# Row-halved attention scores in one PSUM ring, q and k transposed by DMA from tile 6 on, masks built by VectorE

## The chip, the cores and the metric

One core of a Trainium2 chip. The metric is the device time of one execution in microseconds. In a run on a chip, the kernel to be judged and the kernel before are executed in turn on the same chip. A **ratio** is the mean time of one kernel's fast runs over that of the other's fast runs of the same rounds, so it is not quite the ratio of the medians that stand beside it. The span of a profile, from the first to the last instruction, is about 2 us shorter than the time.

## The reference, cut to what matters

```python
scores = (q @ k.T) / sqrt(64) - slope[h] * dist      # B=4, H=8, S=768, D=64
keep   = (pos_k < 8) | ((0 <= rel) & (rel < 96))     # 8 global keys, a window of 96
a      = softmax(where(keep, scores, -1e9))
x      = (a @ v) as [B*S, 512]
out    = relu(x @ w_in)**2 @ w_out                   # w_in [512, 2048], w_out [2048, 512]
```

The 3072 rows are 24 tiles of 128. A tile's queries see only the keys of their own tile and of the one before (the 8 global keys are copied into the latter). Two tiles make a block of the second part; "s1" is x @ w_in in eight steps a block (its result is `hT`), "s2" the product with w_out, "pv" the product a @ v. In the first three tiles a "mask product" adds the distance term to the scores.

## The kernel before: the parts that matter

The kernel plans its own order. Every piece of work is an `op` with a cost, its dependencies and the ring buffer that it takes; a list scheduler puts the pieces in an order, and each engine then executes its own instructions strictly in that order. Some instructions are emitted directly, before the plan:

```python
nc.vector.memset(zero.bitcast(I32), 0)
for j in range(NT):                                   # 24 tiles
    nc.vector.memset(v_sb[j][:, :, D : D + 1], 1.0)   # column of ones beside v
make_identity(nc, ident)
load_qk(1)                                            # loads go out on POOL's queue
...                                                   # masks by POOL
load_v(0)
load_v(1)
nc.vector.tensor_copy(ident32, ident)
```

`v_sb[j]` holds 8 heads of 64 values and a 65th column of ones, with which the product `a @ v` gives the softmax's sum as well.

Scores take one product for a pair of heads: `kT` has both heads' keys on 128 partitions, `qz` has the queries in two halves padded with zeros.

```python
nc.tensor.matmul(out=sc[:, i, :, :], lhsT=kT[kj][:, p_, :],
                 rhs=qz[zi][:, p_, :, :], ...)        # 128 rows x 256 columns
```

TensorE transposes q, k and x for tiles 0 to 9, DMA transposes do it from tile 10 on. PSUM is split: 2 banks of accumulators, 3 of `hT`, 2 of scores, 1 of `po`.

The softmax here doesn't subtract the row's maximum and nothing guards it: scores larger than these inputs give would overflow.

Of the kernel before, what the change touches and what calls it, by code (L numbers as in the profile page):

```python
# [22 lines left out]
class Plan:  # L23
# [7 lines left out]

    LAG = {"PE": 0.25, "ACT": 0.15, "DVE": 0.12, "SP": 2.6, "POOLQ": 2.5, "DMA": 0.0}

# [16 lines left out]
    def run(self):  # L50
        rings = {}
        free = {e: 0.0 for e in self.LAG}
# [10 lines left out]
        while ready:  # L63
            best = None
            for o in ready:
                at = o["at"]
                if o["takes"]:
                    tag, bufs, users = o["takes"]
                    ring = rings.setdefault(tag, [])
                    if len(ring) >= bufs:  # L70
                        old = ring[-bufs]
                        if any("end" not in u for u in old):
                            continue
                        at = max([at] + [self.after(u, o["engines"]) for u in old])
                for e, cost in o["engines"].items():
                    r = (max(at, free[e]), o["key"], cost, o["n"])
                    if best is None or r < best[0]:
                        best = (r, o, e)
# [3 lines left out]
            o["start"], o["engine"], o["end"] = r[0], e, r[0] + o["engines"][e]  # L82
            free[e] = o["end"]
            if o["takes"]:
                rings[o["takes"][0]].append(o["takes"][2])
# [12 lines left out]
def kernel(  # L98
# [32 lines left out]
    NG = NBLK * NSTEP  # L131
    NACC = 2
    NPLAIN = 1
    NFIRST = 4
    NBIAS = 3
    JQK, JX = 10, 10
    NQ, NPAD, NKT, NQZ = 10, 8, 2 * TPB, 4
# [4 lines left out]
    ps_h = ctx.enter_context(tc.tile_pool(name="ps_h", bufs=5 - NACC, space=PSUM))  # L142
    ps_sc = ctx.enter_context(tc.tile_pool(name="ps_sc", bufs=2, space=PSUM))
    ps_o = ctx.enter_context(tc.tile_pool(name="ps_o", bufs=1, space=PSUM))
# [5 lines left out]
    q_ring = [const([P, d_model], BF16, f"q_{i}") for i in range(NQ)]  # L150
    q_pad = [const([P, NPAIR, 2, P], BF16, f"qpad_{i}") for i in range(NPAD)]
    k_ring = [const([P, d_model], BF16, f"k_{i}") for i in range(NQ)]
    v_sb = [const([P, H, D + 1], BF16, f"v_{j}") for j in range(NT)]
    kT = [const([P, NPAIR, P], BF16, f"kT_{i}") for i in range(NKT)]
    qz = [const([P, NPAIR, 2, P], BF16, f"qz_{i}") for i in range(NQZ)]
# [4 lines left out]
    E = const([P, NPAIR, 2, 2, P], BF16, "E")  # L160
    E0 = const([P, NPAIR, 2, P], BF16, "E0")
# [4 lines left out]
    zero = const([P, 4 * P], BF16, "zero")  # L166
    plan = Plan()
    NHS = 14
    E_AT = 14.0
    NWARM = 8  # L170
    HOLD = {}
# [4 lines left out]
    clock = [4.2]  # L176
# [8 lines left out]
    def swdge(name, dst, src, t):  # L185
        nc.gpsimd.dma_start(out=dst, in_=src)  # L186
        clock[0] += t
        land[name] = clock[0]

    q_tile, k_tile = {}, {}  # L190
    for j in range(NPLAIN):
        for n, src in (("q", q), ("k", k)):
            t_ = const([P, d_model], FP32, f"plain_{n}{j}")
            nc.sync.dma_start(
                out=t_.rearrange("p (h d) -> p h d", h=H),
                in_=src_rows(src, j).rearrange("h p d -> p h d"),
            )
            (q_tile if n == "q" else k_tile)[j] = t_
            land[n, j] = 4.1 + 2.1 * j + (1.05 if n == "k" else 0.0)


    def load_v(j):
        swdge(("v", j), v_sb[j][:, :, :D], src_rows(v, j).rearrange("h p d -> p h d"), 0.85)

    def load_qk(j):
        k_tile[j] = k_ring[j % NQ]
        todo = [("k", k_tile[j], k)]
        if j < JQK:
            q_tile[j] = q_ring[j % NQ]
            todo.insert(0, ("q", q_tile[j], q))  # L210
        else:
            q_tile[j] = q_pad[j % NPAD]
            s_ = src_rows(q, j).rearrange("(a e) p d -> e p a d", e=2)
            for e in range(2):
                swdge(("q", j), q_tile[j][:, :, e, e * D : (e + 1) * D], s_[e], 0.43)
        for n, dst, src in todo:
            swdge(
                (n, j), dst.rearrange("p (h d) -> p h d", h=H),
                src_rows(src, j).rearrange("h p d -> p h d"), 0.85,
            )  # L220

    def load_tile(j):
        load_qk(j)
        load_v(j)
# [17 lines left out]
    for j in range(NT):  # L242
        nc.vector.memset(v_sb[j][:, :, D : D + 1], 1.0)
    make_identity(nc, ident)
    load_qk(1)


    nc.gpsimd.iota(pbi, pattern=[[-P, 2], [-1, P]], base=0, channel_multiplier=1)
    nc.gpsimd.tensor_copy(pb, pbi)
    nc.gpsimd.affine_select(  # L250
        out=pb, in_=pb, compare_op=Alu.is_ge, fill=MASK_VAL,
        base=0, pattern=[[P, 2], [1, P]], channel_multiplier=-1,
    )
    nc.gpsimd.affine_select(
        out=pb, in_=pb, compare_op=Alu.is_ge, fill=MASK_VAL,
        base=n_local - 1, pattern=[[-P, 2], [-1, P]], channel_multiplier=1,
    )
    load_v(0)
    load_v(1)
    nc.vector.tensor_copy(ident32, ident)  # L260
    nc.vector.memset(qz[0].bitcast(I32), 0)
    nc.vector.memset(qz[1].bitcast(I32), 0)
    for h in range(H):
        nc.vector.tensor_scalar_mul(sid[h], ident, float(slopes[h] / scale))
    nc.vector.tensor_copy(pb0, pb[:, 0, :])
    nc.vector.tensor_scalar_max(
        pb0[:n_global, :], pb0[:n_global, :], float(-n_local)
    )
    nc.vector.memset(pb[:n_global, 1, :], float(-n_local))
    nc.vector.memset(qz[2].bitcast(I32), 0)  # L270
    nc.vector.memset(qz[3].bitcast(I32), 0)

    warm = ps_o.tile([P, 4 * P], FP32, name="warm", tag="po")
    for i in range(NWARM):
        nc.tensor.matmul(out=warm, lhsT=zero[:, :P], rhs=zero, start=True, stop=True)

    load_tile(2)
    load_w_in(0)
    load_tile(3)
    load_w_out(0)  # L280
    for w in range(1, NSTEP):
        load_w_in(w)
        load_w_out(w)
        if w in (3, 5):
            load_tile(NFIRST + (w - 3) // 2)
# [9 lines left out]
    def any_copy(e, dst, src):  # L295
        if e == "ACT":
            nc.scalar.copy(dst, src)  # L297
        else:
# [4 lines left out]
            ("E", pair), {"ACT": 0.65}, key=0.3 + pair, ready=E_AT,  # L303
            emit=lambda e, pair=pair: [
                nc.scalar.activation(
                    E[:, pair, :, h, :], pb, Act.Exp, scale=float(slopes[2 * pair + h])
                )
                for h in range(2)
            ],
        )  # L310
        for pair in range(NPAIR)
    ]

    def emit_E0(e, c):

        pairs = slice(2 * c, 2 * c + 2)
        nc.vector.tensor_copy(E0[:, pairs], E[:, pairs, 0])
        nc.vector.tensor_max(  # L318
            E0[:n_global, pairs], E[:n_global, pairs, 0], E[:n_global, pairs, 1]
        )  # L320
# [3 lines left out]
            ("E0", c), {"DVE": 0.6}, emit=lambda e, c=c: emit_E0(e, c), key=4 + c,  # L324
            deps=maskE[2 * c : 2 * c + 2],
        )
        for c in range(2)
# [3 lines left out]
    qz_users = [[] for _ in range(NQZ)]  # L331
    kT_users = [[] for _ in range(NKT)]
    qk_users = [[] for _ in range(NQ)]
    pad_users = [[] for _ in range(NPAD)]
# [5 lines left out]
    for j in range(NT):  # L340
# [3 lines left out]
        base = need - LEAD + 4 * (j % 2)  # L344


        if j in late:
            def emit_load(e, j=j):
                if j == JQK:
                    for i in range(NPAD):  # L350
                        nc.gpsimd.memset(q_pad[i].bitcast(I32), 0)
                load_tile(j)
            ld = plan.op(
                ("load", j), {"POOLQ": 2.6}, emit_load,
                deps=qk_users[j % NQ] + (pad_users[j % NPAD] if j >= JQK else []),
                key=base, ready=clock[0],
            )
            qk_users[j % NQ] = []
            if j >= JQK:
                pad_users[j % NPAD] = []  # L360
# [3 lines left out]
        zi, ki = j % NQZ, j % NKT  # L364
        fp = j < NPLAIN
        parts = []
        for n in ("q", "k") if j < JQK else ():
            users = []

            def emit_tr(e, j=j, n=n, fp=fp):  # L370
                pool, tag = ps_h, "hT"
                tr = pool.tile([P, NPAIR, P], FP32 if fp else BF16, name=f"tr{n}", tag=tag)
                src = (q_tile if n == "q" else k_tile)[j]
# [8 lines left out]
                ("tr", n, j), {"PE": 0.85 if fp else 0.24}, emit_tr,  # L382
                deps=[land[n, j]], key=base, ready=HOLD.get(j, 0.0),
                takes=("hT", 5 - NACC, users),
            )
            users.append(tr)
            if n == "q":
                for e_ in range(2):
                    half = slice(e_ * D, (e_ + 1) * D)

                    def emit_z(e, j=j, e_=e_, half=half, zi=zi):
                        any_copy(e, qz[zi][half, :, e_, :], tiles["tr", "q", j][half])

                    z = plan.op(
                        ("z", e_, j), {"DVE": 0.7 if fp else 0.43, "ACT": 0.57}, emit_z,
                        deps=[tr] + qz_users[zi], key=base + 0.1,
                    )
                    users.append(z)
                    parts.append(z)
            else:  # L400
                def emit_T(e, j=j, n=n, ki=ki):
                    any_copy(e, kT[ki], tiles["tr", n, j])

                c = plan.op(
# [412 lines left out]
```

## Time and profile before

| | before |
|---|---|
| time, median of 3 runs | 225.9 us (225.72 to 226.42) |
| span of the profiled run | 223.7 us |
| TensorE busy | 211.1 us, 94% |
| VectorE, ScalarE busy | 146.1 us, 123.3 us |
| granted TensorE clock, mean | 0.989 |

Lines of the timeline: the columns are start, duration, engine, source line, operation and tiles.

TensorE's first useful product starts at 4.21.

### The profile page before, as it was taken

Reading aid. Unit: us, or ns where it says so; the run is one execution under the profiler, and the core shown is the slowest. Engines: PE = TensorE matmul, PEld = TensorE weight load, DVE = VectorE, ACT = ScalarE, POOL = GpSimd, SP = SyncE. Lnnn points to the kernel's source line nnn. Section 1 sums busy time; section 2 is a strip of 40 time slices with the busy share of each in tenths; the row PEclk is TensorE's granted clock in tenths of the full one; section 3 lists DMA queues with packets and bytes.
Section 4 is the critical chain, followed back from the end, with each engine's and each line's share of the span. In section 5 each row is a group of like instructions: output and inputs, shape, how many; then the busy total and the mean of one; then the engine's idle time right before and its main releaser. Section 6 shows DMA issues by size and latency. Waiting matters only on the chain.

```text
span 223.7 us, 4803 instructions
## 1 busy us (share of the span) xinstructions
PE 211.1 (94%) x1817; PEld 151.9 (68%) x1848; DVE 146.1 (65%) x380; ACT 123.3 (55%) x225; POOL 88.0 (39%) x118
## 2 busy tenths in 40 slices
PE   6499999999999999999999999999999999999992
PEld 2388677765777777766767777776776676676750
DVE  6466857677766868757666866866756856844530
ACT  3359666674755944645644745734645644643530
POOL 8996677799978985505605000000000000000000
PEclk9979999999999999999999999999999999999998
DMA  9999999999999999998999984256524430300202
GB/s 132 102 148 199 183 197 180 175 174 169 167 146 151 152 171 169 134 214 98 163 166 129 124 118 95 67 124 95 143 54 90 131 70 13 117 11 17 94 0 94
DMA packets 115142, 27.83 MB, mean 124 GB/s; under 512 B 105776, under 2 KB 112176, under 8 KB 115120
## 3 DMA queue, kind: packets, MB, share of 16 engines
q0 software_dynamic: 79424, 13.38, 79.5%
q1 hardware_dynamic: 35696, 14.16, 32.6%
q8 instruction: 14, 0.23, 0.4%
q14 instruction: 8, 0.07, 0.1%
HBM read 27.26 MB, written 6.29 MB: 150 GB/s over the span
## 4 chain that ended last, share of the span: by engine, by line
PE 82%; POOL 6%; DVE 4%; DMA 4%; ACT 2%; issue 1%; POOLq 0%
PE acc L723 35%; PE hT L659 35%; PE sc L442 7%; PE po L549 4%; DMA win<-in_moe_w_in_dram 4%; DVE hs L692 2%; POOL v L186 1%; POOL q L186 1%; POOL k L186 1%; ACT hr L680 1%; DVE o L299 1%; POOL win L186 1%; PE trx L611 1%; POOL wout L186 1%; ACT qz L297 1%
## 5 line engine op out<-in xcount | busy, mean ns | idle before, releaser
L659 PE MATMUL hT<-xT,win 128*128 128x256 bf16 x768 | 98.6, 273 | 0.5 <-ACT xT L297 0.4
L680 ACT ACTIVATE hr<-hT 128x512 f32<-128x512 f32 x96 | 57.3, 597 | 74.7 <-PE hT L659 72.7
L723 PE MATMUL acc<-wout,hs 128*128 128x512 bf16 x353 | 94.8, 379 | 1.6
L659 PEld LDWEIGHTS <-win 128*128 128x128 bf16 x768 | 74.7, 98 | 23.4 <-DMA win<-in_moe_w_in_dram 0.7
L692 DVE TENSOR_TENSOR hs<-hr 128x512 bf16<-128x512 f32 x96 | 65.9, 687 | 25.7 <-ACT hr L680 24.3
L723 PEld LDWEIGHTS <-hs 128*128 128x128 bf16 x384 | 34.5, 98 | 22.8
L482 ACT ACTIVATE esc<-sc 128x512 bf16<-128x512 f32 x78 | 46.2, 593 | 2.4 <-PE sc L442 2.3
L442 PE MATMUL sc<-qz,kT 128*128 128x256 bf16 x176 | 35.3, 276 | 0.7 <-ACT at L482 0.4
L503 DVE TENSOR_TENSOR at<-esc,E 128x512 bf16<-128x512 bf16 x78 | 32.4, 417 | 0.1
L186 POOL DMA_DIRECT2D qpad<-in_q_dram x28 | 21.6, 800 | 23.0 <-DMA qz<-qpad 23.0
L186 POOL DMA_DIRECT2D v<-in_v_dram x24 | 22.0, 918 | 2.6 <-DVE E L318 1.7
L186 POOL DMA_DIRECT2D k<-in_k_dram x23 | 21.2, 920 | 3.1 <-PE trx L611 1.8
L575 DVE TENSOR_TENSOR x<-po,rs 128x256 bf16<-128x256 f32 x48 | 20.4, 424 | 1.7
L549 PEld LDWEIGHTS <-at 128*128 128x128 bf16 x352 | 17.2, 99 | 5.9
L574 DVE RECIPROCAL rs<-po 128x4 f32<-128x4 f32 x48 | 8.7, 180 | 18.2 <-PE po L549 17.6
L442 PEld LDWEIGHTS <-kT 128*128 128x128 bf16 x176 | 17.1, 99 | 3.1 <-DVE kT L299 0.8
L549 PE MATMUL po<-v,at 128*128 128x65 bf16 x352 | 18.8, 194 | 0.0
L299 DVE COPY o<-acc 128x512 f32<-128x512 f32 (+1 forms) x12 | 8.0, 664 | 8.2 <-PE acc L723 4.3
L297 ACT COPY o<-acc 128x512 f32<-128x512 f32 (+1 forms) x13 | 7.4, 570 | 5.3 <-PE acc L723 5.2
L297 ACT COPY qz<-trq 64x512 bf16<-64x512 bf16 x10 | 5.8, 580 | 7.5 <-DVE qz L299 5.3
L522 DVE COPY kT<-kT 128x32 bf16<-128x32 bf16 x16 | 3.4, 210 | 9.2 <-PE sc L442 9.2
L186 POOL DMA_DIRECT2D q<-in_q_dram x9 | 8.3, 924 | 1.5 <-DMA wout<-in_moe_w_out_dram 1.2
(52 smaller groups left out, 91.2 us busy)
## 6 DMA issues: line engine op xcount, KB each, us to landing
out_dram<-o SPq DMA_DIRECT2D x23, 256.0 KB, 2.5
v<-in_v_dram POOLq DMA_DIRECT2D x24, 128.0 KB, 6.7
k<-in_k_dram POOLq DMA_DIRECT2D x23, 128.0 KB, 5.7
win<-in_moe_w_in_dram POOLq DMA_DIRECT2D x8, 256.0 KB, 8.4
wout<-in_moe_w_out_dram POOLq DMA_DIRECT2D x8, 256.0 KB, 8.8
qpad<-in_q_dram POOLq DMA_DIRECT2D x28, 64.0 KB, 4.5
q<-in_q_dram POOLq DMA_DIRECT2D x9, 128.0 KB, 7.9
plain_q<-in_q_dram SPq DMA_DIRECT2D x1, 256.0 KB, 3.3
```

Of the source, the lines that this page charges most:

```text
L186: nc.gpsimd.dma_start(out=dst, in_=src)
L297: nc.scalar.copy(dst, src)
L299: nc.vector.tensor_copy(dst, src)
L442: nc.tensor.matmul(out=sc[:, i, :, :], lhsT=kT[kj % NKT][:, p_, :], rhs=qz[zi][:, p_, :, :], start=True, stop=j >= NBIAS, skip_group_check ...
L482: nc.scalar.activation(out=esc, in_=sc.rearrange("p a b c -> p (a b c)"), func=Act.Exp, scale=scale,)
L503: nc.vector.tensor_mul(at, tiles.pop(("esc", j, pair)), bias.rearrange("p a b c -> p (a b c)"))
L549: nc.tensor.matmul(out=po[:, hi, :], lhsT=at[:, pair % 2 if first else i, h % 2, :], rhs=v_sb[kj][:, h, :], start=(i == 0), stop=(i == len ...
L575: nc.vector.tensor_tensor(out=x[:, 4 * hf : 4 * hf + 4, :], in0=po[:, :, :D], in1=rs.to_broadcast([P, 4, D]), op=Alu.mult,)
L659: nc.tensor.matmul(out=hT[:, c, :], lhsT=w_in_sb[s][:, kt, c * P : (c + 1) * P], rhs=tiles["xT", blk][:, kt, :], start=(kt == 0), stop=(kt ...
L680: nc.scalar.activation(hr, tiles.pop(("hT", blk, s)), Act.Relu)
L692: nc.vector.tensor_mul(hs, hr, hr)
L723: nc.tensor.matmul(out=tiles["acc", blk, sub], lhsT=hs[:, c, sub * P : (sub + 1) * P], rhs=w_out_sb[s][:, c, :], start=(s == 0 and c == 0) ...
```

## The change

Its intent: halve TensorE's time on the scores, take transposes from TensorE, and start sooner, by taking masks and identity from POOL so that it issues loads earlier. The diff is cut to its core:

```diff
-    JQK, JX = 10, 10
-    NQ, NPAD, NKT, NQZ = 10, 8, 2 * TPB, 4
+    JQK, JX = 6, 6                 # DMA transposes of q,k / of x from this tile on
+    NQ, NKT = 6, 2 * TPB           # six load buffers
+    NG = 8 - NACC                  # one ring of 6 PSUM banks: scores, po, hT, transposes
...
     nc.vector.memset(zero.bitcast(I32), 0)
-    for j in range(NT):
-        nc.vector.memset(v_sb[j][:, :, D : D + 1], 1.0)
-    make_identity(nc, ident)
-    load_qk(1)
+    load_part(0, 1)
     nc.gpsimd.iota(pbi, ...)
+    load_part(1, 1)
     load_v(0)
     load_v(1)
...
+    for j in range(4):
+        nc.vector.memset(v_sb[j][:, :, D : D + 1], 1.0)
+    nc.vector.tensor_scalar(ident32, pbi[:, 0, :], 0.0, None, op0=Alu.is_equal)
...                                 # masks by VectorE
+    for g in range(4, NT, 5):      # the other twenty, in four planned groups
+        js = range(g, min(g + 5, NT))
+        o = plan.op(("ones", g), {"DVE": 0.2}, lambda e, js=js: emit_ones(e, js),
+                    key=4.0 * g - 20, ready=15.0)
...                                 # order of the first loads changed: w_in earlier
-                    nc.tensor.matmul(out=sc[:, i, :, :], lhsT=kT[kj % NKT][:, p_, :],
-                                     rhs=qz[zi][:, p_, :, :], ...)
+                for odd in range(2):
+                    half = slice(odd * D, (odd + 1) * D)
+                    nc.tensor.matmul(out=sc[odd, g][:, at, :],
+                                     lhsT=qkT[(j - kt) % NKT][half, 1, pair, :],
+                                     rhs=qkT[j % NKT][half, 0, pair, :], ...)
```

From tile 4 on all score products of a tile go out in one burst: sixteen into four banks of the ring, or eight into two in a tile that starts a batch.

## The prediction

> **What bounds the kernel now.** I read the page's busy shares and its chain first, then its groups, then the stretches by window, then the transfers.
>
> ```profile
> PE 211.1 (94%) x1817; PEld 151.9 (68%) x1848; DVE 146.1 (65%) x380; ACT 123.3 (55%) x225; POOL 88.0 (39%) x118
> ...
> PE 82%; POOL 6%; DVE 4%; DMA 4%; ACT 2%; issue 1%; POOLq 0%
> ...
> L659 PE MATMUL hT<-xT,win 128*128 128x256 bf16 x768 | 98.6, 273 | 0.5 <-ACT xT L297 0.4
> ...
> L723 PE MATMUL acc<-wout,hs 128*128 128x512 bf16 x353 | 94.8, 379 | 1.6
> ...
> L442 PE MATMUL sc<-qz,kT 128*128 128x256 bf16 x176 | 35.3, 276 | 0.7 <-ACT at L482 0.4
> ```
>
> TensorE is the bound, and no other engine is near it. The mean of a matmul (273 ns) contains the latency, so I take what a product adds in a stream from start to start in the timeline: two score products of 256 columns take 0.22 us before the next group starts (109 ns each), eight s1 products 0.87 us, two s2 products of 512 columns 0.43 us, eight pv products of 65 columns 0.24 us (29.6 ns, with their weight loads), four bf16 transposes 0.23 us (57 ns). Summed over the whole program: s1 768 x 0.109 = 83.7, s2 384 x 0.216 = 82.9, scores 176 x 0.109 = 19.2, pv 352 x 0.0296 = 10.4, mask products 40 x 0.057 = 2.3, bf16 transposes 112 x 0.057 = 6.4, eight fp32 transposes 1.2: **206.1 us of slots**. From the first useful product (4.2 us) to the last one's end (219.5) are 215.3 us, so only 9.2 us are lost. Where?
>
> ```profile
> 4.20:11.00 6.80, 2.93 (x31) 2.27 (x31) 3.06 (x9) 2.73 (x5) 6.66 (x10) 0.98 1.74 112
> 11.00:15.00 4.00, 4.00 (x47) 3.68 (x48) 2.11 (x7) 2.15 (x4) 4.00 (x7) 0.62 1.81 148
> 15.00:19.50 4.50, 3.71 (x62) 3.30 (x59) 3.26 (x12) 3.52 (x8) 4.33 (x7) 1.00 1.66 177
> ...
> 60.00:80.00 20.00, 19.84 (x186) 14.54 (x187) 14.05 (x35) 13.97 (x26) 17.90 (x24) 1.00 2.07 166
> ```
>
> The first pair of numbers after the stretch is its length and PE's busy time; the third from the end is the granted clock. From 60 us on PE is idle for under 1%. The start holds the loss: 3.9 us idle in 4.2 to 11, then 4 us at a granted clock of 0.62 (1.5 us lost), 0.8 us idle in 15 to 19.5. The idle piece that matters is one line of the timeline:
>
> ```profile
> 10.91 0.61 PE L375 MATMUL trq<-ident,q 128*128 128x128 bf16 x4 [2.27 <-DMA q<-in_q_dram]
> ```
>
> PE stood 2.27 us in its program order before the transposes of tile 2's q, which had not landed, and the slow clock follows at once.
>
> **What the Trainium skill says.** "TensorE: Matmul & The Clock Gate", section "Back-to-back issue gap": an isolated gap is N/2.4 + 2.5 ns; that is 109, 56 and 29.6 ns for 256, 128 and 65 columns, and the trace agrees with all three (109, 57, 29.6). Its Part 1 says that an idle window of about 3.4 us returns the array to half clock; the 0.62 after the wait above fits, though that wait was shorter. "TensorEngine Tiling (Array Packing)", section "Key Properties": row tiles run in parallel, and changing the tiling mode drains TensorE; the kernel before never does this, so no number here shows either. "DMA: Bandwidth & Descriptors", section "Queues, rings and completion order": a DMA engine takes turns between queue rows packet by packet, so a transpose shares with the loads; the trace agrees, see the 9.2 us below.
>
> **The change part by part.**
> (1) Scores. A head pair was one product of 128 rows against 256 columns, half of them zeros: 109 ns. Now each head has a product of 64 rows by 128 columns, even heads on rows 0 to 63, odd heads on 64 to 127, into different banks. If the two row halves overlap, a pair costs about 56 ns, so 28 to 29 ns a product, which the pv rate shows that weight loads can follow. 352 x 0.029 = 10.2 us instead of 19.2. Against this stands a change of tiling mode into and out of each burst. A product's tail beyond its slot is 273 - 109 = 164 ns; if each of the two changes exposes up to that, a burst costs 0 to 0.33 us extra; I choose 0.25. The program order of the changed kernel has 27 bursts (one in tile 0, two each in tiles 1 to 3, one in every later tile): 6.8 us. So 10.2 + 6.8 = 17.0: **-2.2 us**, with -9.0 if a change costs nothing, and about 0 at 0.33.
> (2) Transposes. TensorE now transposes q and k only for tiles 0 to 5 and x only for tiles 0 to 5, instead of up to 9: four tiles x 12 = 48 fewer, x 0.057 = **-2.7 us**. Their PSUM copies leave ACT and DVE, which wait anyway. The slots fall to 201.2 us.
> (3) The start. Only an iota is left on POOL between the loads, so the third load is issued about 1.9 us sooner; q2's transposes now stand behind all of tile 1's scores, which takes the 2.27 us wait and probably the slow clock. Before, the first s1 started at 19.38 us with 8.4 us of slots done. In the new order 8.2 us of slots precede it; with some 3 us of waits (tile 3's q lands at about 15) that is near 15.5. So PE gains 3 to 4 us here, if nothing takes it back.
> (4) The ring. Scores take four of six shared banks; in the new order 2.6 us of s1 and s2 follow each burst before the first pv product, and two exps and a relu on ACT need 3 x 0.6 us, two multiplications 0.42 us each. I expect little waiting, up to 1 us in all.
>
> **The rivals.** *The first transposed tile comes late.* Before, tile 6 was transposed by TensorE at 49.23 us; now its q and k have to land and then go through a DMA transpose while the loads of tiles 7 to 11 fill the queues.
>
> ```profile
> k<-in_k_dram POOLq DMA_DIRECT2D x1, 128.0 KB, 8.3
> ...
> qz<-qpad SPq DMA_TRANSPOSE x1, 9.2
> ```
>
> The first is tile 6's k, issued at 35.98 and so landed at 44.3; the second is the first DMA transpose of before, at 59.7, under full load (the same transpose later takes 3.3 us, xT's 2.4). The loads ahead of tile 6 are the same, and the queue was never idle after 10 us, so k lands only by what the start gains, about 1.9 us: 42.4. A transpose of 5 to 9 us puts tile 6's scores at 48 to 52, I choose 49.8. In the new order 36.5 us of slots stand before them: PE would be there at 4.2 + 36.5 + 4 = 44.7, or at about 46 because the last w_out (landed at 42.6 before, 33.8 + 8.8, now about 40.8) is needed at 31.2 us of slots. So PE waits about 4 us, and the gain of the start is lost. Then: before, tile 6's first score stood at 51.2 with 206.1 - 38.2 = 167.9 us of slots to go; now at 49.8 with 201.2 - 36.5 = 164.7. That is -1.4 - 3.2 = -4.6 us, less 1 us if the clock halves after the wait: 221.3 to 222.3 us. Against it: the planner of the new kernel was evidently set by someone who saw traces and chose tile 6.
> *It comes in time.* Then (44.7 - 51.2) - 3.2 = -9.7, less a us for ring waits: about 217.
> *Tiling changes are free, or dear.* Of the 27 bursts 18 lie after tile 6's start; free makes 4.5 us less, 0.33 us each makes 1.4 us more. The fixed 0.25 in the new planner's PE figure for a score burst speaks for an observed cost, but I don't use it as a time.
> *The row halves do not overlap* (56 ns a product): 352 x 0.056 = 19.7 us plus the changes, some 10 us more, so 230. The separate banks and the whole layout speak against it.
>
> **Range and chances.** I give 60% to the late tile 6 (-4.1 with half of the clock loss) and 40% to a start that keeps its gain (-8.7): -5.9 us, so 220.0. The cost of a tiling change shifts this by -4 to +1.4, the wait by 2 us each way: 215.5 to 224.5. The line of 2% is 221.4, between the two cases: faster 0.62, same 0.34, slower 0.04.
>
> **What would show it.** The score group's 352 products with starts 28 to 29 ns apart, and a gap of about 0.12 us on entering and leaving a burst; scores' share of the chain down; the first s1 near 15.5 us; a PE wait before tile 6's scores ended by the DMA qkT<-qk, with a landing of 5 to 9 us; from 60 us on still under 1% idle. I am wrong if starts are 56 ns apart, if tile 6's transpose lands before 45 us, if hT products wait on exps for ring banks, or if the start is still waiting for q2.

## More of the kernel before

```profile
1.11 0.70 DVE L243 MEMSET v<- 128x8 bf16 x19
...
4.21 0.62 PE L375 MATMUL trq<-ident,plain_q 128*128 128x128 f32 x4
```

The memsets of the ones columns run back to back at 1.1 us, before any load of v has been issued, and wait for nothing.

## The result, and the profile after

The changed kernel takes **244.24 us** (median of 4 runs, 243.18 to 245.92) against 225.81 for the kernel before in the same rounds: ratio 1.0817 (1.0751 to 1.0884). It is 8% slower, and the prediction (220.0, range 215.5 to 224.5) was wrong.

First the page of the changed kernel: busy times, and the chain that ended last by engine.

```profile
PE 209.8 (87%) x1944; PEld 144.3 (60%) x1976; DVE 142.7 (59%) x369; ACT 117.8 (49%) x215; POOL 73.9 (31%) x91
...
PE 66%; DMA 18%; POOL 6%; issue 4%; DVE 2%; ACT 1%; SPq 0%; POOLq 0%
```

No engine is busier than before. The chain has lost TensorE (82% to 66%) and won DMA (4% to 18%): something waits for transfers. The windows show where (columns: length, then the busy time of PE, PEld, DVE, ACT and POOL, the granted clock, DMA share, GB/s):

```profile
4.20:11.00 6.80, 1.49 (x7) 0.91 (x5) 1.21 (x9) 0.00 (x0) 4.37 (x6) 1.00 1.99 149
...
25.00:30.00 5.00, 0.55 (x11) 0.41 (x9) 0.00 (x0) 0.81 (x2) 3.81 (x5) 1.00 1.90 176
30.00:35.00 5.00, 0.00 (x0) 0.00 (x0) 0.07 (x1) 0.00 (x0) 3.11 (x5) 0.50 1.61 187
35.00:40.00 5.00, 0.72 (x9) 0.48 (x10) 2.08 (x12) 0.08 (x1) 3.54 (x5) 0.50 1.59 192
40.00:45.00 5.00, 4.78 (x33) 3.03 (x33) 3.10 (x9) 3.54 (x9) 4.06 (x5) 0.64 2.10 168
...
60.00:80.00 20.00, 19.79 (x171) 12.87 (x174) 13.61 (x37) 10.48 (x20) 7.10 (x9) 1.00 1.48 157
```

From 30 to 35 us TensorE, VectorE and ScalarE all stand still, while the loads go on. TensorE's timeline names its three great waits:

```profile
10.09 1.97 PE L370 MATMUL tr<-ident,plain 128*128 128x128 f32 x8 [5.31 <-DVE ident L250]
...
39.27 0.29 PE L428 MATMUL sc<-qkT 64*128 64x128 bf16 x2 [13.72 <-DVE qkT L302]
...
122.40 0.68 PE L541 MATMUL po<-v,at 128*128 128x65 bf16 x4 [3.70 <-DVE at L499]
```

Each is put down to VectorE. But VectorE is busy for 59% only, so the question is what VectorE waited for:

```profile
7.99 0.07 DVE L249 MEMSET v<- 128x8 bf16 x1 [6.85 <-DMA v<-in_v_dram]
...
30.07 0.07 DVE L275 MEMSET v<- 128x8 bf16 x1 [7.62 <-DMA v<-in_v_dram]
37.85 0.07 DVE L275 MEMSET v<- 128x8 bf16 x1 [7.71 <-DMA v<-in_v_dram]
...
121.89 0.07 DVE L275 MEMSET v<- 128x8 bf16 x1 [6.60 <-DMA v<-in_v_dram]
```

This is the main cause, in four lines: memsets of 65 ns that waited 6.6 to 7.7 us each for a load of v. In these four the memset of a tile's ones column comes after the load of that tile's v in the program. The two write different columns, but the same tile, and the built program makes the later write wait for the earlier one's semaphore. "TensorE: Matmul & The Clock Gate" in the Trainium skill says in Part 1, under engine queue depths, that ScalarE and VectorE are strict FIFO; the trace agrees: the copies of q and k, the normalizations and the squares behind the memset all stood until 37.85, although their inputs had long been there. The memsets of tiles 4 and 5 were planned for 15 us at a cost of 0.2, with no dependency on the load.

The order holds the other way round too. In the program the memset of tile 2's v stands before the load of tile 2's v, so POOL could not issue that load until VectorE had come through. This is POOL's line in the changed kernel and then in e1, the first experiment below, where nothing holds it:

```profile
10.23 0.96 POOL L189 DMA_DIRECT2D v<-in_v_dram  x1 [2.43 <-DVE ident L251]
```

```profile
7.81 0.92 POOL L189 DMA_DIRECT2D v<-in_v_dram  x1
```

The trace names VectorE's instruction next to the memset (the memsets of tiles 1 to 3 run at 9.84); that it is the memset is read from the program and from e1 and e2, where the load goes out at 7.81. Every later load stands behind this one in POOL's queue.

The row-halved scores themselves do what they were meant to do. One burst of sixteen in the changed kernel (starts in the first column):

```profile
49.15 0.29 PE L604 MATMUL trx<-ident,x 128*128 128x128 bf16 x2 [0.40 <-DVE x L569]
49.37 0.23 PE L428 MATMUL sc<-qkT 64*128 64x128 bf16 x2
49.43 0.22 PE L428 MATMUL sc<-qkT,qkT 64*128 64x128 bf16 x2
...
50.11 1.91 PE L652 MATMUL hT<-xT,win 128*128 128x256 bf16 x16
```

Two products in 0.057 us are 28.5 ns each, where a full one of this width takes 57. Two transposes end their slots at 49.15 + 0.11 = 49.26, so entering the burst cost about 0.1 us. The `hT` products at 50.11 waited for a copy of xT by ScalarE that ended at 50.06, so the way out is not read here. In the burst of eight at 21.93 us of the same trace both ways are free: 0.09 us in and 0.09 us out.

### The profile page after: what moved, and what is told of

It is laid out like the page before. It is cut to its first block, busy times and chain, and to the rows that moved or that the text cites. A ratio compares the mean times of both kernels' runs of the same rounds, so it can differ in the third digit from the quotient of the medians.

```text
span 242.1 us, 4972 instructions
## 1 busy us (share of the span) xinstructions
PE 209.8 (87%) x1944; PEld 144.3 (60%) x1976; DVE 142.7 (59%) x369; ACT 117.8 (49%) x215; POOL 73.9 (31%) x91
## 4 chain that ended last, share of the span: by engine, by line
PE 66%; DMA 18%; POOL 6%; issue 4%; DVE 2%; ACT 1%; SPq 0%; POOLq 0%
PE hT L652 30%; PE acc L716 29%; DMA v<-in_v_dram 7%; DMA qkT<-qk 5%; DMA wout<-in_moe_w_out_dram 4%; PE sc L428 4%; POOL qk L189 4%; PE po L541 3%; DMA qk<-in_k_dram 2%; POOL win L189 1%; DVE hs L685 1%; POOL v L189 1%; ACT hr L673 1%; POOL wout L189 1%; PE trx L604 0%
## 5 line engine op out<-in xcount | busy, mean ns | idle before, releaser
L716 PE MATMUL acc<-wout,hs 128*128 128x512 bf16 x352 | 91.4, 382 | 2.5 <-DVE hs L685 0.6
L652 PEld LDWEIGHTS <-win 128*128 128x128 bf16 x768 | 71.7, 99 | 17.2 <-issue 0.2
L474 ACT ACTIVATE esc<-sc 128x512 bf16<-128x512 f32 x78 | 42.3, 597 | 30.9 <-PE sc L428 30.9
L716 PEld LDWEIGHTS <-hs 128*128 128x128 bf16 x384 | 37.5, 99 | 30.7 <-DVE hs L685 1.2
L189 POOL DMA_DIRECT2D qk<-in_q_dram x23 | 20.8, 904 | 69.4 <-DMA qkT<-qk 64.6
L428 PE MATMUL sc<-qkT 64*128 64x128 bf16 x192 | 13.9, 227 | 14.9 <-DVE qkT L302 14.6
L428 PEld LDWEIGHTS <-qkT 64*128 64x128 bf16 x352 | 10.4, 97 | 24.6 <-DVE qkT L302 15.1
L189 POOL DMA_DIRECT2D qk<-in_k_dram x23 | 20.7, 902 | 0.5 <-DMA wout<-in_moe_w_out_dram 0.5
L428 PE MATMUL sc<-qkT,qkT 64*128 64x128 bf16 x160 | 12.0, 223 | 0.0
L474 ACT ACTIVATE at<-sc 128x512 bf16<-128x512 f32 x10 | 5.4, 594 | 4.8 <-PE sc L438 4.7
```

What stands on the lines that cost most here:

```text
L189: nc.gpsimd.dma_start(out=dst, in_=src)
L428: nc.tensor.matmul(out=sc[odd, g][:, at, :], lhsT=qkT[(j - kt) % NKT][half, 1, pair, :], rhs=qkT[j % NKT][half, 0, pair, :], start=True, s ...
L474: nc.scalar.activation(out=esc, in_=tiles.pop(("sc", j, odd, g)).rearrange("p a c -> p (a c)"), func=Act.Exp, scale=scale,)
L652: nc.tensor.matmul(out=hT[:, c, :], lhsT=w_in_sb[s][:, kt, c * P : (c + 1) * P], rhs=tiles["xT", blk][:, kt, :], start=(kt == 0), stop=(kt ...
L716: nc.tensor.matmul(out=tiles["acc", blk, sub], lhsT=hs[:, c, sub * P : (sub + 1) * P], rhs=w_out_sb[s][:, c, :], start=(s == 0 and c == 0) ...
```

## The experiments

All ten passed the comparison with the reference. e7 computes wrong scores, and its output still stayed within the tolerance.

**Is it the memsets, and which?** Rivals: the memsets only fill slack, and the scores or the ring cost the time; or the memsets cost, but behind them tile 6's late DMA transpose waits, as the prediction had it.

*e1_ones_first*: all 24 memsets before any load; the planned pieces stay in the plan but emit nothing, so every other instruction keeps its order.

```diff
     nc.vector.memset(zero.bitcast(I32), 0)
+    for j in range(NT):
+        nc.vector.memset(v_sb[j][:, :, D : D + 1], 1.0)
...
-    for j in range(4):
-        nc.vector.memset(v_sb[j][:, :, D : D + 1], 1.0)
...
-            ("ones", g), {"DVE": 0.2}, lambda e, js=js: emit_ones(e, js),
+            ("ones", g), {"DVE": 0.2}, None,
```

> Changed kernel, but all 24 memsets of the ones column of v issued before any load (as the kernel before has them); the order of every other instruction is kept. Theory A (the memsets behind the loads of v in DVE's order cost the time): PE's waits of 5.3 us (to 10.1), 13.7 us (to 39.3) and 3.7 us (to 122.4), and the slow clock after each, go. What then remains is the lateness of tile 6's DMA transpose (landed 44.6 + 8.3 = 52.9 in the changed kernel), so PE should now wait some 5 us before tile 6's scores, until about 52, and the time be 221 to 224 us. Theory B (memsets cost, and tile 6's transpose costs nothing): 216 to 219 us. Theory C (the row-halved scores or the ring are the cost, the memsets only absorb slack): above 235 us.

Measured: 224.47 us (before 226.13), ratio 0.9919 (0.9859 to 0.998): just above the 221 to 224 of theory A, and far from B and C. The three waits are gone, and one large one is left. TensorE's timeline and two windows of e1:

```profile
46.48 0.81 PE L716 MATMUL acc<-wout,hs 128*128 128x512 bf16 x3
51.85 0.61 PE L428 MATMUL sc<-qkT 64*128 64x128 bf16 x8 [4.57 <-DMA qkT<-qk]
```

```profile
45.00:50.00 5.00, 2.23 (x13) 0.97 (x12) 0.60 (x2) 0.00 (x0) 4.76 (x6) 1.00 2.26 145
50.00:60.00 10.00, 8.10 (x59) 5.39 (x61) 3.96 (x9) 2.88 (x5) 2.91 (x4) 0.83 1.95 167
```

Some 20 us of the changed kernel were the memsets. What remains is the prediction's first rival: the scores of tile 6 wait until 51.85 for a DMA transpose issued at 43.40 that took 8.4 us beside the loads, and the clock drops after it.

*e2_first4*: only the first four memsets moved up.

```diff
     nc.vector.memset(zero.bitcast(I32), 0)
+    for j in range(4):
+        nc.vector.memset(v_sb[j][:, :, D : D + 1], 1.0)
...
-    for j in range(4):                                # behind the loads of v 0, v 1
-        nc.vector.memset(v_sb[j][:, :, D : D + 1], 1.0)
```

> Only the first four memsets moved before the loads. Theory A: the 5.3 us wait before the first transposes and the slow clock to 19 us go, but the weights and tile 5's v land no sooner, so DVE's wait for tile 5's v (until about 37.9) holds PE as before: only a little is gained by the end, 240 to 244 us. If the waits simply add: 234 to 237 us. Theory C: 244.

Measured: 244.13 us, ratio 1.079 (1.0728 to 1.0851): nothing gained. Theory C expected 244 here too, so this run alone would not tell A from C; e1 does. TensorE of e2:

```profile
37.23 0.29 PE L428 MATMUL sc<-qkT 64*128 64x128 bf16 x2 [18.77 <-DVE qkT L302]
```

The work that starts 5 us sooner arrives sooner at the same wall. Tile 5's v lands when the queue of loads has come that far (VectorE goes on at 35.8 instead of 37.85, as POOL is no longer held at the start), so the second wait grew from 13.72 to 18.77 us. Waits before one late transfer do not add.

*e3_late20*: only the late twenty moved up, the first four stay behind the loads.

```diff
     nc.vector.memset(zero.bitcast(I32), 0)
+    for j in range(4, NT):
+        nc.vector.memset(v_sb[j][:, :, D : D + 1], 1.0)
...
-            ("ones", g), {"DVE": 0.2}, lambda e, js=js: emit_ones(e, js),
+            ("ones", g), {"DVE": 0.2}, None,
```

> Only the late twenty memsets (tiles 4 to 23) moved before the loads, the first four stay behind the loads of v 0 and v 1. Theory A: PE still starts at about 10, but no longer stands at 25.5 to 39.3; the late start is then partly hidden behind the weights and tile 6's transpose, which set the pace until 52: 223 to 228 us. If the waits simply add (244 - 13.7 - 3.7 - clock): 222 to 226. Theory C: above 235.

Measured: 226.28 us, ratio 1.0005 (0.9973 to 1.0036). TensorE of e3:

```profile
10.87 1.97 PE L372 MATMUL tr<-ident,plain 128*128 128x128 f32 x8 [6.36 <-DVE ident L252]
...
53.99 0.40 PE L430 MATMUL sc<-qkT 64*128 64x128 bf16 x8 [3.61 <-DMA qkT<-qk]
```

A start that is 6 us late costs only 1.8 us against e1, because tile 6's transpose sets the pace afterwards. The 1.8 us fit the loads: POOL is held for 3.20 us before v of tile 2 (issued at 11.01, in e1 at 7.81), tile 6's transpose is issued at 45.84 instead of 43.40, and TensorE goes on 2.1 us later than in e1. So of the 20 us, the late memsets are some 18.

*r1_before_ones_late*: the reverse test. In the kernel before, the loop of memsets is moved behind `load_v(0)` and `load_v(1)`, nothing else.

```diff
-    for j in range(NT):
-        nc.vector.memset(v_sb[j][:, :, D : D + 1], 1.0)
...
     load_v(0)
     load_v(1)
+    for j in range(NT):
+        nc.vector.memset(v_sb[j][:, :, D : D + 1], 1.0)
```

> The kernel before with its loop of 24 memsets moved behind the loads of v 0 and v 1, nothing else. Theory A: DVE waits for both loads (about 8 to 12 us) before it makes the fp32 identity, PE's first transposes move from 4.2 us to 10 us or later, and the time goes up by 4 to 8 us, 230 to 234 us. If such memsets are harmless: 226 us.

Measured: 233.02 us, ratio 1.0305 (1.0264 to 1.0345): a loop of memsets moved by some lines costs the old kernel 7 us. VectorE of r1:

```profile
8.83 0.07 DVE L259 MEMSET v<- 128x8 bf16 x1 [7.70 <-DMA v<-in_v_dram]
10.31 0.67 DVE L259 MEMSET v<- 128x8 bf16 x18 [1.42 <-DMA v<-in_v_dram]
10.94 0.67 DVE L260 CAST ident<-ident 128x128 f32<-128x128 bf16 x1
```

The fp32 identity, made at 1.77 us before, is now made at 10.94, and TensorE's first transposes start at 11.66. POOL is held here too (2.11 us before v of tile 2, issued at 10.71 instead of 8.60). How the 7 us divide between the late identity and the later loads is not shown.

**Is the rest tile 6, and what do the scores really cost?** All four start from e1.

*e4_tr_to_8*: TensorE transposes q and k of tiles 6 and 7 too. A second edit tells the planner of a later landing, which can move other pieces; no run separates the two.

```diff
-    JQK, JX = 6, 6
+    JQK, JX = 8, 6
...
-                key=base, ready=issue[0],
+                key=base, ready=issue[1] - 3.0,
```

> The mended kernel of the first run (all memsets first), with q and k of tiles 6 and 7 transposed by TensorE too (the DMA transposes start with tile 8), and the planner told of a later landing so that these transposes stand where the data is there. Theory A (what is left is the wait for tile 6's DMA transpose, 4.57 us, and some 1.3 us of slow clock after it): both go, 16 transposes of 57 ns are added (0.9 us): 224.5 - 5.9 + 0.9 = 219.5, say 218 to 221 us. Rival (the transfers as a whole are late, so the wait moves to tile 8 or to the loads): 222 to 225 us.

Measured: **219.63 us** (219.62 to 219.91; before 225.88), ratio 0.972 (0.9693 to 0.9746). The wait is gone. TensorE of e4 waits between 30 and 100 us for 0.83 and 0.17 us, both for xT:

```profile
69.53 1.05 PE L652 MATMUL hT<-xT,win 128*128 128x256 bf16 x8 [0.83 <-DMA xT<-x]
```

*e5_tr_to_7*: the same with `JQK, JX = 7, 6`.

> As the run with DMA transposes from tile 8 on, but from tile 7 on. Tile 7's q and k land at about 46, its transpose some 8 us later at 54; its scores stand 8 us of slots after tile 6's, at 54 to 56 us. Theory A: no wait or under 1 us, so the same time as from tile 8 on within 1 us. Rival: a wait of several us before tile 7's scores, 2 us or more slower.

Measured: 220.17 us, ratio 0.974 (0.9708 to 0.9771), 0.5 us above e4. That is small, but the five runs (220.12 to 221.47) do not overlap e4's four. Tile 7's scores wait 0.33 us at 56.3 in the profiled run, which is the slowest of the five and also waits 1.06 us for a w_out. So the DMA transposes could begin with tile 7 at about that cost, but not with tile 6.

*e6_split_bursts*: e4 with two bursts of eight products a tile.

```diff
-    NSPLIT = 4
+    NSPLIT = NT
```

> As the run with DMA transposes from tile 8 on, but every tile's scores in two bursts of eight products instead of one of sixteen: 44 bursts instead of 27, the same 352 products. If a change of tiling into and out of a burst costs the 0.19 us read from the trace: +17 x 0.19 = +3.2 us over that run. If it costs nothing: the same time, or less, as only two banks are taken at once.

Measured: 222.85 us, ratio 0.9855 (0.9826 to 0.9885): 3.2 us above e4 for 17 more bursts, so 0.19 us a burst. The order of other pieces changes a little with it (its waits between 30 and 220 us, the usual last one aside, are 0.5 us or less each), so this is the size, not an exact cost.

*e7_full_rows*: wrong scores, e4's order: each score product takes all 128 rows, so that it sums both heads of the pair.

```diff
-                    half = slice(odd * D, (odd + 1) * D)
+                    half = slice(0, P)
```

> Wrong results on purpose: as the run with DMA transposes from tile 8 on, same program order, but each of the 352 score products takes all 128 rows (both heads summed) by 128 columns, so no row tiling. If the row halves overlap (28.5 ns a product in the trace, against 57 ns for a full product): 352 x 0.057 = 20.1 us instead of 10.0 + 27 x 0.19 = 15.2, so +4.9 us over that run. If the overlap is not real (the modelled ends hide it): the same or faster, by up to 5 us.

Measured: 223.03 us, ratio 0.9868 (0.9841 to 0.9896), 3.4 us above e4. The burst of eight products of the same tile, one that starts a batch, in e7 and then in e4:

```profile
97.48 0.61 PE L428 MATMUL sc<-qkT 128*128 128x128 bf16 x8
97.92 1.04 PE L652 MATMUL hT<-xT,win 128*128 128x256 bf16 x8
```

```profile
96.83 0.40 PE L428 MATMUL sc<-qkT 64*128 64x128 bf16 x8
97.16 1.05 PE L652 MATMUL hT<-xT,win 128*128 128x256 bf16 x8
```

Full products: 0.44 us to the next start (8 x 55 ns). Halves: 0.33, that is 8 x 28.5 ns and 0.10 for the way out. The overlap is real. The time rose by 3.4 instead of 4.9: e7, being later, no longer meets the two waits for xT (1.0 us) in the middle; the remaining half us I did not trace.

**A little more?**

*f1_x_to_8*: e4 with `JQK, JX = 8, 8`, x of tiles 6 and 7 transposed by TensorE.

> The best so far (q and k transposed by TensorE through tile 7, all memsets first), with x of tiles 6 and 7 transposed by TensorE too. In that run PE waited 0.83 and 0.17 us for the DMA transposes xT<-x; the eight added transposes cost 8 x 0.057 = 0.46 us. If both waits go: 219.6 - 1.0 + 0.5 = 219.1, inside its noise. If the waits return at tile 8: 219.6 to 220.2.

Measured: 219.4 us (219.28 to 219.51), ratio 0.9711 (0.9692 to 0.9729). The waits for xT are gone, and the gain is not clear of e4's.

*f2_order*: f1 with the first loads in another order.

```diff
-    for w in "i0 T2 i1 T3 i2 o0 ...".split():
+    for w in "T2 i0 T3 i1 i2 o0 ...".split():
```

> The same with tile 2's q, k, v loaded ahead of the first w_in, and w_in 1 behind tile 3 as before. The waits for q and k of tile 2 (0.42 + 0.49 us at 11.4 to 12.4) and for q of tile 3 (0.91 us at 16.2) were the largest at the start; w_in 0 is needed only after tile 3's q. If tile 2 lands 1.3 us sooner these shrink by about 1 us: 218 to 218.5 us. If the loads as a whole set the pace of the first 40 us, nothing is gained: 219 us.

Measured: 219.71 us, ratio 0.9714 (0.9694 to 0.9735): no gain. The waits for tile 2 vanish, and others take their place (1.47 us for tile 3's k at 16.5, 0.98 for w_out at 26.6). This fits the loads as a whole pacing the first 30 us.

f1 beats both kernels: 3% faster than before, 10% faster than the changed one.

## Why the prediction was wrong, point by point

- **The step that failed is (3), "The start"**, with the 4 us of waits that the first rival allows TensorE on its way to tile 6. The prediction counted what leaves POOL and never followed VectorE's own order, where 24 memsets had moved from before the loads to behind some of them. It expected a gain of 3 to 4 us and a first s1 near 15.5. In the changed kernel TensorE starts at 10.09 instead of 4.21, the first s1 at 22.94, and a wait of 13.7 us follows before 39.27. The whole loss by the memsets is some 20 us (changed kernel against e1), and some 18 of it are the late twenty (e3). The earlier loads failed with it: v of tile 0 went out at 3.52 instead of 5.11 (1.6 us sooner; 1.9 was predicted), but v of tile 2 at 10.23 instead of 8.60. The diff's line "ones" with 0.2 us on VectorE looked like nothing, yet the diff shows that the memset of v 0 now stands behind the load of v 0 and ahead of the identity.
- **(3), the mended start.** In e4 the first s1 starts at 16.42 us (19.38 before; about 15.5 was predicted), and the wait for tile 2's q is 0.42 us instead of 2.27. Its slow clock is gone in e4, but e1 has one at 15 to 18 us with waits of at most 0.77 us before it, so the reading that the one long wait brings it is not borne out. But the gain at the start does not reach the end: span less slots is 223.7 - 206.1 = 17.6 us before and 218.0 - 200.3 = 17.7 in e4 (its slots: 199.4 with the measured score costs, and 0.9 for 16 transposes). After the first s1 TensorE's listed waits sum to 3.0 us in e4 and 0.9 before. Of the 3.0, 1.0 are for loads (at 24 to 28 us) and 1.0 for the two DMA transposes of x.
- **(1) Scores: right, a term mis-sized.** 28.5 ns a product held. A burst costs 0.19 us beyond its products by the trace and by e6, not 0.25. So 352 x 0.0285 + 27 x 0.19 = 15.2 us instead of 17.0; the gain is 4.0 us where 2.2 was predicted.
- **(2) Transposes: right in direction**, not isolated by a run; with only tiles 6 and 7 given back, e4's gain of 6.2 us over before agrees with slots that fall by 5.8, scores and transposes together.
- **(4) The ring: right as far as the traces show.** From 60 to 100 us the changed kernel has no wait of PE that the trace lists, and e4's two are for a DMA transpose.
- **The rival "the first transposed tile comes late": right, hidden in the changed kernel.** There TensorE came so late that tile 6 was ready. In e1 PE arrived at 47.3 (predicted 46) and went on at 51.85 (predicted 49.8): the transpose was issued at 43.40 (42.4 was predicted) and took 8.4 us where 7.4 was chosen. e1 stands at 224.5, slow clock included, where the rival gave 221.3 to 222.3.
- **The chances** rested on two cases, with "slower" at 0.04: every case assumed that nothing but TensorE's order and the transfers mattered.

## What to carry to other kernels

When an instruction moves in program order, ask what it now comes behind: two 65 ns memsets, each behind a load that writes the same tile, on an engine that works in order, held three engines for 14 us. Ask the same for what now comes behind it: a load may wait for the memset. Initialize the parts of a tile that no load writes before the loads are issued, or keep them in a tile of their own (not tried here). And judge a wait by the next wall behind it: mending the first wait alone gained nothing (e2), mending the last alone nearly everything (e3).

## What the Trainium skill lacked or had wrong

- "TensorEngine Tiling (Array Packing)", "Key Properties", says that a change of tiling mode drains TensorE, without a size. Here it costs about 0.1 us into and 0.1 us out of a burst (0.19 us a burst by e6), and 64-row products of 128 columns then start 28.5 ns apart, with their own weight loads.
- "TensorE: Matmul & The Clock Gate", "Back-to-back issue gap", gives 81 ns (N = 128) and 131 ns (N = 512) for sustained streams with weight loads and calls N/2.4 + 2.5 the isolated case. In these streams the second form holds: 57 and 216 ns.
- The same page, Part 1: half clock after an idle window of about 3.4 us. The kernel before fell to 0.62 after a wait of 2.27 us; its transposes ran 100 ns apart from 10.91 on. The prediction called this a fit; 2.27 us is short of the window. Nor does the length of one wait decide in these runs: in e1 the clock was 0.56 in 15 to 18 us after waits of at most 0.77 us, while waits up to 0.91 us in e4 had no such effect. What sets it off stays open. Its caveat that trace records of the clock can be unreliable fits: between 10.1 and 19.4 us the changed kernel's mask products ran 103 ns apart instead of 57, with a recorded clock of 1.00.
- "DMA: Bandwidth & Descriptors" gives the turn-taking of queues but no latency of a transpose beside loads: 256 KB took 8.2 to 10.7 us then (changed kernel and e1, 40 to 60 us), 3.3 us in the quiet part of the kernel before.
- No page warns that writes to disjoint columns of one tile by a load and by an engine are kept in order by the build, so that the later one waits: 6.6 to 7.7 us in the changed kernel for memsets of 65 ns, and 2.43 us for a load behind a memset.
